# VectorE's share of the attention exponentials, computed on the bit pattern of the bf16 result

## The chip, the cores and the metric

One core of one Trainium2 chip runs the whole program. A time is device microseconds (us) from start to end of one execution. Each execution also lists the mean clock that was granted to TensorE over its span, as a share of full speed; that column matters below. An execution over 1.5% above the fastest of the same kernel counts as slow, and ratios leave it out.

## The reference

```python
x = A_q                                              # 1 x 2048 x 640, bf16
g = sigmoid((x * gate_w).sum(-1, keepdims=True))
a = _A_ref(x, A_k, A_v, ...)    # 4-tap shift of k, times v, long convolution by FFT of length 4096, skip, times q
b = _B_ref(x, wq, wk, wv, wo)   # attention, 32 query heads of 20, one shared key/value head:
#   scores = einsum("bhqd,bkd->bhqk", q, k) * 20 ** -0.5 ;  p = softmax(scores) ;  o = p @ v ;  b = o @ wo
return g * a + (1 - g) * b
```

The attention has 32 x 2048 x 2048 = 134 million scores, each of which needs an exponential. That is what the kernel is built around.

## The kernel before

The kernel is a Python program that lists operations and hands them to a list scheduler of its own. When the kernel is built, this scheduler fixes the order of every engine's instructions, from durations that it models. The stream of score matmuls, exponentials and value matmuls (P times V) has precedence. Everything else is "side work" in its gaps: the convolution (as products with cosine and sine tables), the projections, the output products.

ScalarE takes most exponentials, alternately from three score banks (ETA) and two (ETB):

```python
def EXP(n):
    lo, w = 512 * base[n % 2], 512 * len(units[n])
    op("act", lambda e: e.activation(et(n)[:, 0:w], self.ps[:, lo:lo + w], ACT.Exp, scale=SCALE), ...)
```

VectorE takes 66 pairs of 512-column tiles (a list named DVE_J says which). It evacuates scores as a scaled integer J. The bits of J above the low 16 are the exponent of the result, and the low 16 are the position within the octave, on which a cubic in factored form is computed:

```python
def DEXP(G, j):
    ...
        self.evac(gr, "dve", lambda e, bk, h=h: e.tensor_scalar(        # twice, one per score bank
            J[:, 512 * h:512 * h + 512], self.bank(bk), SCALE * LOG2E * 65536.0, EOFF * 65536.0, ALU.mult,
            ALU.add), (), [kJ], c_ps(512))
    V(lambda e: e.tensor_scalar(E[:, :], J[:, :], 7, 0x7F800000, ALU.logical_shift_left, ALU.bitwise_and), ...)
    V(lambda e: e.scalar_tensor_tensor(Ef, lo, ED, Ef, ALU.add, ALU.mult), ...)
    V(lambda e: e.scalar_tensor_tensor(Jf, lo, EP, lo, ALU.add, ALU.mult), ...)
    V(lambda e: e.scalar_tensor_tensor(T["ETd"][:, :], Jf, EQ, Ef, ALU.add, ALU.mult), ...)
```

One more part matters, and it is in the scheduler. Where nothing is ready for TensorE, it may place a "dummy" matmul. A dummy adds zero weights times anything to the output bank (bank 6), so it changes no result ("fill" and "filler" in the code):

```python
FILL = 0.55
...
if best is None:                                   # no side work is ready for TensorE
    if (self.filler is not None and self.main_started and self.can_fill and m is not None and gap > 0.1
            and self.busy_in(t, 2.4) < FILL):      # modelled activity of the last 2.4 us
        f = Op("pe", self.filler, c_mm(512), "c", "fill", 0.0)
...
if op.name == "pv":
    self.can_fill = not op.last                    # no dummy between the last PV of a group and the next group's first
```

Of the kernel before, what the change touches and what calls it, by code (L numbers as in the profile page):

```python
# [5 lines left out]
dt = mybir.dt  # L6
# [495 lines left out]
CW = 128  # L502
HD = 320

C3 = 0.0780245226404771
ED, EP, EQ = 1.8383391255622578 * 2.0 ** 16, 1.0590468215349557 * 2.0 ** 16, 6.971251820088461 * 2.0 ** 32
EOFF = 127.0 - 48.0 + math.log2(C3)
LOG2E = 1.4426950408889634

UP = 256.0  # L510

# [6 lines left out]
def c_ps(n):  # L518
    return 0.16 + 1.04e-3 * n


def c_fast(n):
    return 0.16 + 0.52e-3 * n
# [10 lines left out]
def c_pool(n):  # L534
    return 0.21 + 1.78e-3 * n
# [6 lines left out]
class Kernel:  # L542
# [59 lines left out]
    def alloc(self):  # L602
# [3 lines left out]
        def sb(name, shape, dtype):  # L606
            T[name] = nc.alloc_sbuf_tensor(name, shape, dtype)
# [29 lines left out]
            sb(f"ETA{i}", [128, 1536], BF16)  # L637
            sb(f"ETB{i}", [128, 1024], BF16)
        sb("ETd", [128, 1024], BF16)
        sb("dJ0", [128, 1024], dt.uint32)  # L640
        sb("dJ1", [128, 1024], dt.uint32)
        sb("dE", [128, 1024], dt.uint32)
        sb("kv", [128, NSC, D], BF16)
        sb("xn", [128, NSC, D], BF16)
        sb("ident", [128, 128], BF16)
# [368 lines left out]
    def attention(self):  # L1014
        T = self.T
        op = self.op
        self.stream()
        units = self.units
        base = (0, 3)
# [39 lines left out]
        def DEXP(G, j):  # L1059

            par = self.ndexp % 2
            self.ndexp += 1
            pr = -600.0 + 0.1 * G + 0.001 * j
            J, E, kJ = T[f"dJ{par}"], T["dE"], ("dJ", par)
            lo = J[:, :].bitcast(dt.uint16).rearrange("p (n t) -> p n t", t=2)[:, :, 0]
            Ef, Jf = E[:, :].bitcast(F32), J[:, :].bitcast(F32)
            k = dict(port=True, name="dexp", prio=pr)
            V = self.dve
            rs = self.on_dve[G, j]
            for h, r in enumerate(rs):  # L1070
                gr = self.group("dqk", pr, banks=(5, 7))
                gr.rides = True

                w = self.g.writer.get(kJ)
                soft = set() if h else set(self.g.readers.get(kJ, ())) | ({w} if w is not None else set())
                self.mm(gr, lambda e, bk, r=r: score(e, bk, G, j, r), [("kT4", j // 4), ("qT", G // 8 % 2, G % 8)],
                        0.04)
                o = gr.mms[0]
                o.row = r
                if self.dqk is not None:  # L1080
                    o.deps.add(self.dqk)
                self.dqk = o
                o.soft = soft - o.deps
                o.deps |= o.soft
                self.evac(gr, "dve", lambda e, bk, h=h: e.tensor_scalar(  # L1085
                    J[:, 512 * h:512 * h + 512], self.bank(bk), SCALE * LOG2E * 65536.0, EOFF * 65536.0, ALU.mult,
                    ALU.add), (), [kJ], c_ps(512))
            V(lambda e: e.tensor_scalar(E[:, :], J[:, :], 7, 0x7F800000, ALU.logical_shift_left, ALU.bitwise_and),  # L1088
              [kJ], ["dE"], c_fast(1024), **k)
            V(lambda e: e.scalar_tensor_tensor(Ef, lo, ED, Ef, ALU.add, ALU.mult), [kJ, "dE"], ["dE"], c_ps(1024),  # L1090
              **k)
            V(lambda e: e.scalar_tensor_tensor(Jf, lo, EP, lo, ALU.add, ALU.mult), [kJ], [kJ], c_ps(1024), **k)  # L1092
            V(lambda e: e.scalar_tensor_tensor(T["ETd"][:, :], Jf, EQ, Ef, ALU.add, ALU.mult), [kJ, "dE"], ["ETd"],  # L1093
              c_ps(1024), **k)

        def PVmm(r, j, src, key, late=False, **k):
            return op("pe", lambda e: e.matmul(  # L1097
                self.bank(6)[32 * r:32 * r + 32, :], T["vaug"][:, j, :], src,
                start=(j == 0), stop=(j == NSC - 1), tile_position=(0, 32 * r)),
                [key, "vaug", ("vaugb", j // 4)], [] if late else [("ps", 6)], name="pv", **k)  # L1100

        def PV(G, j, rs):
            pv0 = None
# [91 lines left out]
    def tail(self):  # L1195

        T = self.T
        acc, g = T["acc"], 7
        v = lambda t: t[:, :].rearrange("p (b r) -> p b r", r=32)
        p = -9000.0  # L1200
        self.dve(lambda e: e.transpose(acc[:, :], self.bank(6)), [("ps", 6)], ["acc"], c_ps(512), prio=p, name="tp")
        self.dve(lambda e: e.reciprocal(T["rcp"][:, :], v(acc)[:, :, 20]), ["acc"], ["rcp"], 0.3, prio=p, name="rcp")
        self.dve(lambda e: e.tensor_tensor(v(T["oTn"]), v(acc), T["rcp"][:, :].unsqueeze(2).to_broadcast([128, 16, 32]),
                                           ALU.mult), ["acc", "rcp"], ["oTn"], c_ps(512), prio=p, port=True,
                 name="onorm")
        self.dve(lambda e: e.transpose(T["oT3"][:, g, :], T["oTn"][:, :]), ["oTn"], [("oT3", g)], c_ps(512), prio=p,
                 name="tp")

        def mm(ci, half, g):
            b, n0 = 2 * ci + half, HD * half  # L1210
            self.op("pe", lambda e: e.matmul(
                self.bank(b, HD), T["oT3"][:, g, 128 * ci:128 * ci + 128], T["wog"][:, g, n0:n0 + HD],
                start=(g == 6), stop=(g == 7)), [("oT3", g), "wog"], [("ps", b)], c_mm(HD), name="op2", main=True,
                banks=(b,))

        def warm():

            self.op("pe", lambda e: e.matmul(self.bank(0, HD), T["zeros"][:, :], T["wog"][:, 6, 0:HD], start=False,
                                             stop=False), ["zeros", "wog"], [("ps", 0)], c_mm(HD), name="warm",
                    main=True, banks=(0,))  # L1220

        for ci in range(4):
            for half in range(2):
                mm(ci, half, 6)
            if ci >= 2:
                for _ in range(6):
                    warm()
        for ci in range(4):
            i = 4 * (NB - 1) + ci
            osb = T[f"outsb{ci}"]  # L1230
            for half in range(2):
                mm(ci, half, 7)
            self.dve(lambda e, ci=ci, i=i, osb=osb: e.scalar_tensor_tensor(
                osb[:, :].rearrange("p (h n) -> p h n", h=2),
                self.ps[:, 1024 * ci:1024 * ci + 1024].rearrange("p (h n) -> p h n", h=2)[:, :, 0:HD],
                T["omgf"][:, i:i + 1], T["part"][:, ci, :].rearrange("p (h n) -> p h n", h=2), ALU.mult, ALU.add),
                ["omgf", ("ps", 2 * ci), ("ps", 2 * ci + 1), ("part", ci)], [("outsb", ci)], c_ps(D), prio=p,
                name="op2_ev")
            self.dma(self.aps["out"][0][128 * i:128 * i + 128, :], osb[:, :], reads=[("outsb", ci)],
                     nbytes=163840, prio=p, name="st_out", eng="act" if ci % 2 else "sp")  # L1240
# [300 lines left out]
```

## Time and profile before

| | before |
|---|---|
| three timed executions | 908.10, 911.01, 912.96 us |
| mean granted clock, profiled execution | 0.998 |
| to the first exponential ("head") | 25.30 us |
| first to last start of an exponential ("stream") | 872.65 us |
| after the last start ("tail") | 9.95 us |
| ACT busy, DVE busy, PE busy | 883.9, 631.9, 853.1 of 907.9 us |
| dummy matmuls in the stream, by their weight loads | 149 |

The prediction shows and reads the lines behind this. In profile lines PE stands for TensorE's matmuls, PEld for its weight loads, DVE for VectorE, ACT for ScalarE, POOL for GpSimd. Three rows add up to the span (head, stream, tail), so any change of time must appear in one of them. The stream is nearly the whole of it. What it takes beyond the undisturbed 854.1 us, which the prediction works out, is called its loss here. A caution: most of these traces lack the matmul records of some dummies (before has 111 for its 149 weight loads), so TensorE's busy time is read a little low where dummies stand.

### The profile page before, as it was taken

Reading aid. Unit: us, or ns where it says so; the run is one execution under the profiler, and the core shown is the slowest. Engines: PE = TensorE matmul, PEld = TensorE weight load, DVE = VectorE, ACT = ScalarE, POOL = GpSimd, SP = SyncE. Lnnn points to the kernel's source line nnn. Section 1 sums busy time; section 2 is a strip of 40 time slices with the busy share of each in tenths; the row PEclk is TensorE's granted clock in tenths of the full one; section 3 lists DMA queues with packets and bytes.
Section 4 is the critical chain, followed back from the end, with each engine's and each line's share of the span. In section 5 each row is a group of like instructions: output and inputs, shape, how many; then the busy total and the mean of one; then the engine's idle time right before and its main releaser. Section 6 shows DMA issues by size and latency. Waiting matters only on the chain.

```text
span 907.9 us, 16333 instructions
## 1 busy us (share of the span) xinstructions
PE 853.1 (94%) x6950; PEld 350.7 (39%) x7013; DVE 631.9 (70%) x878; ACT 883.9 (97%) x791; POOL 380.2 (42%) x330
## 2 busy tenths in 40 slices
PE   6999999999999999999999999999999998998897
PEld 3344344443433344343333333343443332432233
DVE  5446743456766668876887778876678896787964
ACT  5999999999999999999999999999999999999995
POOL 2940056870426396154685213769125495000000
PEclk9999999999999999999999999999999999999999
DMA  7940300010000010000010200000000000301111
GB/s 162 200 134 9 65 19 20 7 37 18 20 19 14 9 41 19 19 19 13 13 37 19 56 20 13 19 8 18 20 19 14 18 4 25 93 13 35 64 35 52
DMA packets 58507, 32.69 MB, mean 36 GB/s; under 512 B 41154, under 2 KB 54466, under 8 KB 58434
## 3 DMA queue, kind: packets, MB, share of 16 engines
q1 hardware_dynamic: 56168, 31.05, 12.7%
q8 instruction: 55, 0.90, 0.4%
q10 hardware_dynamic: 2266, 0.59, 0.3%
q14 instruction: 18, 0.15, 0.1%
HBM read 18.01 MB, written 6.02 MB: 26 GB/s over the span
## 4 chain that ended last, share of the span: by engine, by line
ACT 64%; PE 29%; DMA 3%; SPq 2%; DVE 2%; issue 1%; DVEq 0%
ACT ETA L1055 39%; ACT ETB L1055 25%; PE ps L1023 8%; PE ps L1336 6%; PE ps L1097 6%; PE ps L1400 3%; PE ps L949 2%; PE ps L1270 1%; DMA kTr<-in_A_k_dram 1%; SPq L1253 1%; DMA rbc<-scr_d 1%; DMA xT<-in_A_q_dram 1%; PE ps L1434 1%; PE ps L1187 1%; SPq L722 1%
## 5 line engine op out<-in xcount | busy, mean ns | idle before, releaser
L1055 ACT ACTIVATE ETA<-ps 128x1536 bf16<-128x1536 f32 x384 | 571.3, 1488 | 3.5 <-PE ps L1097 2.2
L1055 ACT ACTIVATE ETB<-ps 128x1024 bf16<-128x1024 f32 x383 | 410.3, 1071 | 0.2 <-PE ps L1023 0.2
L1023 PE MATMUL ps<-qT,kT 21*128 21x512 bf16 x2048 | 302.5, 384 | 34.6 <-ACT ETA L1055 22.7
L1367 POOL TENSOR_TENSOR Pp<-X,K 128x512 f32<-128x512 bf16 x120 | 168.6, 1430 | 358.2 <-DVE K L1355 350.8
L1097 PE MATMUL ps<-ETA,vaug 128*32 128x512 bf16 x1150 | 196.1, 389 | 0.4 <-DVE acc L1151 0.3
L1097 PE MATMUL ps<-ETB,vaug 128*32 128x512 bf16 x766 | 188.1, 389 | 0.0
L1023 PEld LDWEIGHTS ps<-qT,kT 21*128 21x128 bf16 x2048 | 74.7, 91 | 223.2 <-ACT ETA L1055 122.9
L1085 DVE TENSOR_SCALAR dJ<-ps 128x512 uint32<-128x512 f32 x132 | 90.7, 687 | 43.8 <-PE ps L1023 43.4
L1093 DVE SCALAR_TENSOR_TENSOR ETd<-dJ,dE 128x1024 bf16<-128x1024 f32 x66 | 89.4, 1354 | 19.5 <-PE ps L1097 19.4
L1090 DVE SCALAR_TENSOR_TENSOR dE<-dJ,dE 128x1024 f32<-128x1024 uint16 x66 | 89.9, 1362 | 0.5
L1092 DVE SCALAR_TENSOR_TENSOR dJ<-dJ 128x1024 f32<-128x1024 uint16 x66 | 89.3, 1353 | 0.4
L1367 POOL TENSOR_TENSOR AB<-Pp 128x256 bf16<-128x256 f32 x80 | 77.4, 967 | 4.9
L1400 PE MATMUL ps<-AB,Tcos 128*128 128x256 bf16 x320 | 78.2, 275 | 0.8 <-DVE dJ L1085 0.6
L1097 PEld LDWEIGHTS ps<-ETA,vaug 128*32 128x32 bf16 x1150 | 47.7, 93 | 65.6 <-issue 63.0
L1400 PE MATMUL ps<-AB,Tsin 128*128 128x256 bf16 x280 | 69.3, 275 | 0.0
L1097 PEld LDWEIGHTS ps<-ETB,vaug 128*32 128x32 bf16 x766 | 45.3, 92 | 43.5 <-issue 42.9
L1367 POOL TENSOR_TENSOR Pp<-Pp 128x512 f32<-128x512 f32 x40 | 60.9, 1524 | 2.7
L1088 DVE TENSOR_SCALAR dE<-dJ 128x1024 uint32<-128x1024 uint32 x66 | 54.1, 820 | 0.5
L1336 PE MATMUL ps<-ssm_kT,Tsin 128*128 128x256 bf16 x320 | 53.7, 275 | 0.0
L1336 PE MATMUL ps<-kv,Tsin 128*128 128x256 bf16 x320 | 53.7, 275 | 0.0
L1336 PE MATMUL ps<-kv,Tcos 128*128 128x256 bf16 x320 | 52.0, 275 | 1.2 <-DVE kv L1410 0.5
L1336 PE MATMUL ps<-ssm_kT,Tcos 128*128 128x256 bf16 x320 | 51.8, 275 | 0.4 <-DVE dJ L1085 0.3
(135 smaller groups left out, 807.5 us busy)
## 6 DMA issues: line engine op xcount, KB each, us to landing
rbc<-scr_d SPq DMA_DIRECT2D x31, 256.0 KB
scr_o<-oTn SPq DMA_DIRECT2D x24, 128.0 KB, 1.8
xn<-in_A_q_dram SPq DMA_DIRECT2D x4, 640.0 KB
kv<-in_A_v_dram SPq DMA_DIRECT2D x4, 640.0 KB, 5.3
out_dram<-outsb SPq DMA_DIRECT2D x14, 160.0 KB, 1.8
oTp<-scr_o SPq DMA_DIRECT2D x12, 160.0 KB, 5.2
wog<-in_B_wo_dram SPq DMA_DIRECT2D x4, 200.0 KB
wo<-in_B_wo_dram SPq DMA_DIRECT2D x4, 200.0 KB, 3.3
```

The source lines that it names most:

```text
L949: o = self.mm(gr, lambda e, bk, gi=gi, dc=dc: e.matmul(self.bank(bk), T["wq_pad"][:, dc, 128 * gi:128 * gi + 128], T["xT"][:, dc, 512 * I: ...
L1023: return e.matmul(self.bank(bk), T["kT4"][32 * r:32 * r + 21, 128 * j:128 * j + 128], T[f"qT{G // 8 % 2}"][32 * r:32 * r + 21, G % 8, :], ...
L1055: op("act", lambda e: e.activation(et(n)[:, 0:w], self.ps[:, lo:lo + w], ACT.Exp, scale=SCALE), [("ps", base[n % 2] + k) for k in range(le ...
L1085: self.evac(gr, "dve", lambda e, bk, h=h: e.tensor_scalar(J[:, 512 * h:512 * h + 512], self.bank(bk), SCALE * LOG2E * 65536.0, EOFF * 6553 ...
L1088: V(lambda e: e.tensor_scalar(E[:, :], J[:, :], 7, 0x7F800000, ALU.logical_shift_left, ALU.bitwise_and), [kJ], ["dE"], c_fast(1024), **k)
L1090: V(lambda e: e.scalar_tensor_tensor(Ef, lo, ED, Ef, ALU.add, ALU.mult), [kJ, "dE"], ["dE"], c_ps(1024), **k)
L1092: V(lambda e: e.scalar_tensor_tensor(Jf, lo, EP, lo, ALU.add, ALU.mult), [kJ], [kJ], c_ps(1024), **k)
L1093: V(lambda e: e.scalar_tensor_tensor(T["ETd"][:, :], Jf, EQ, Ef, ALU.add, ALU.mult), [kJ, "dE"], ["ETd"], c_ps(1024), **k)
L1097: return op("pe", lambda e: e.matmul(self.bank(6)[32 * r:32 * r + 32, :], T["vaug"][:, j, :], src, start=(j == 0), stop=(j == NSC - 1), ti ...
L1336: o = self.mm(gr, lambda e, bk, lhs=lhs, rhs=rhs, comp=comp, n=n: e.matmul(self.bank(bk, 256, 256 * comp), lhs, rhs, start=(n == 0), stop= ...
L1367: f = lambda e: e.tensor_tensor(out, a, b, alu)
L1400: self.mm(gr, lambda e, bk, lhs=lhs, fc=fc, comp=comp, h=h: e.matmul(self.bank(bk, 256, 256 * h), lhs, AB[:, fc, :, comp, :], start=(fc == ...
```

## The change

The intent is to shorten VectorE's chain from four links after the evacuations to three. The evacuation writes a negative f32, W = 128 x (score in octaves + 44) - 32768. Rounded to int16, W is already a bf16 bit pattern with the sign bit set: an exponential whose fraction is interpolated linearly, negative and too small by 2^83. What is missing is a cubic correction in the position within the octave, and that position can be read off the low 16 bits of W as a float. So shift-and-mask goes. The sign and the 2^83 are made good by a second value tile, vneg, which the products with VectorE's results load in place of vaug.

```diff
+DA = -10.141843429407468 / 2.0 ** 48
+DP = -5.834910002780118 * 2.0 ** 16
+DQ = 4.8360429603910475 * 2.0 ** 32
+KDN = 83
...
+        self.pool(lambda e: e.tensor_scalar(T["vneg"][:, :, :], T["vaug"][:, :, :], -(2.0 ** KDN), 1.0, ALU.mult,
+                                            ALU.mult), ...)
...
-                    J[:, 512 * h:512 * h + 512], self.bank(bk), SCALE * LOG2E * 65536.0, EOFF * 65536.0, ALU.mult,
-                    ALU.add), (), [kJ], c_ps(512))
-            V(lambda e: e.tensor_scalar(E[:, :], J[:, :], 7, 0x7F800000, ALU.logical_shift_left, ALU.bitwise_and),
-            V(lambda e: e.scalar_tensor_tensor(Ef, lo, ED, Ef, ALU.add, ALU.mult), [kJ, "dE"], ["dE"], c_ps(1024),
-            V(lambda e: e.scalar_tensor_tensor(Jf, lo, EP, lo, ALU.add, ALU.mult), [kJ], [kJ], c_ps(1024), **k)
-            V(lambda e: e.scalar_tensor_tensor(T["ETd"][:, :], Jf, EQ, Ef, ALU.add, ALU.mult), [kJ, "dE"], ["ETd"],
+                    W[:, 512 * h:512 * h + 512], self.bank(bk), SCALE * LOG2E * 128.0,
+                    128.0 * (127 - KDN) - 32768.0, ALU.mult, ALU.add), (), [kW], c_ps(512))
+            V(lambda e: e.scalar_tensor_tensor(X[:, :], w, DP, w, ALU.add, ALU.mult), [kW], ["dX"], c_ps(1024), **k)
+            V(lambda e: e.scalar_tensor_tensor(X[:, :], X[:, :], DQ, w, ALU.add, ALU.mult), [kW], ["dX"], c_ps(1024),
+            V(lambda e: e.scalar_tensor_tensor(T["ETd"][:, :].bitcast(dt.int16), X[:, :], DA, W[:, :], ALU.mult,
+                                               ALU.add), [kW, "dX"], ["ETd"], c_ps(1024), **k)
...
+            va = "vneg" if late else "vaug"
-                self.bank(6)[32 * r:32 * r + 32, :], T["vaug"][:, j, :], src,
+                self.bank(6)[32 * r:32 * r + 32, :], T[va][:, j, :], src,
...
+            if g == 6 and ci == 0 and half == 0:         # first output matmul of the tail
+                o.deps.update(x for gr in self.g.groups for x in gr.evacs)
```

The scheduler works from durations, so removing one instruction also moves nearly every side matmul a little, and the dummies with them.

More of the change, by code (lines that the diff above doesn't have):

```diff
@@ L503 @@
 HD = 320
-C3 = 0.0780245226404771
-ED, EP, EQ = 1.8383391255622578 * 2.0 ** 16, 1.0590468215349557 * 2.0 ** 16, 6.971251820088461 * 2.0 ** 32
-EOFF = 127.0 - 48.0 + math.log2(C3)
 LOG2E = 1.4426950408889634
+DA = -10.141843429407468 / 2.0 ** 48
+DP = -5.834910002780118 * 2.0 ** 16
+DQ = 4.8360429603910475 * 2.0 ** 32
+KDN = 83
 UP = 256.0
@@ L639, in alloc @@
         sb("ETd", [128, 1024], BF16)
-        sb("dJ0", [128, 1024], dt.uint32)
-        sb("dJ1", [128, 1024], dt.uint32)
-        sb("dE", [128, 1024], dt.uint32)
+        sb("dW0", [128, 1024], F32)
+        sb("dW1", [128, 1024], F32)
+        sb("dX", [128, 1024], F32)
+        sb("vneg", [128, NSC, 32], BF16)
         sb("kv", [128, NSC, D], BF16)
@@ L1016, in attention @@
         op = self.op
+        self.pool(lambda e: e.tensor_scalar(T["vneg"][:, :, :], T["vaug"][:, :, :], -(2.0 ** KDN), 1.0, ALU.mult,
+                                            ALU.mult), ["vaug"] + [("vaugb", b) for b in range(NB)], ["vneg"],
+                  c_pool(512), prio=14.0, name="vneg", after=self.crow0)
         self.stream()
@@ L1063, in DEXP @@
             pr = -600.0 + 0.1 * G + 0.001 * j
-            J, E, kJ = T[f"dJ{par}"], T["dE"], ("dJ", par)
-            lo = J[:, :].bitcast(dt.uint16).rearrange("p (n t) -> p n t", t=2)[:, :, 0]
-            Ef, Jf = E[:, :].bitcast(F32), J[:, :].bitcast(F32)
+            W, X, kW = T[f"dW{par}"], T["dX"], ("dW", par)
+            w = W[:, :].bitcast(dt.uint16).rearrange("p (n t) -> p n t", t=2)[:, :, 0]
             k = dict(port=True, name="dexp", prio=pr)
@@ L1072, in DEXP @@
                 gr.rides = True
-                w = self.g.writer.get(kJ)
-                soft = set() if h else set(self.g.readers.get(kJ, ())) | ({w} if w is not None else set())
+                wr = self.g.writer.get(kW)
+                soft = set() if h else set(self.g.readers.get(kW, ())) | ({wr} if wr is not None else set())
                 self.mm(gr, lambda e, bk, r=r: score(e, bk, G, j, r), [("kT4", j // 4), ("qT", G // 8 % 2, G % 8)],
@@ L1085, in DEXP @@
                 self.evac(gr, "dve", lambda e, bk, h=h: e.tensor_scalar(
-                    J[:, 512 * h:512 * h + 512], self.bank(bk), SCALE * LOG2E * 65536.0, EOFF * 65536.0, ALU.mult,
-                    ALU.add), (), [kJ], c_ps(512))
-            V(lambda e: e.tensor_scalar(E[:, :], J[:, :], 7, 0x7F800000, ALU.logical_shift_left, ALU.bitwise_and),
-              [kJ], ["dE"], c_fast(1024), **k)
-            V(lambda e: e.scalar_tensor_tensor(Ef, lo, ED, Ef, ALU.add, ALU.mult), [kJ, "dE"], ["dE"], c_ps(1024),
-              **k)
-            V(lambda e: e.scalar_tensor_tensor(Jf, lo, EP, lo, ALU.add, ALU.mult), [kJ], [kJ], c_ps(1024), **k)
-            V(lambda e: e.scalar_tensor_tensor(T["ETd"][:, :], Jf, EQ, Ef, ALU.add, ALU.mult), [kJ, "dE"], ["ETd"],
-              c_ps(1024), **k)
+                    W[:, 512 * h:512 * h + 512], self.bank(bk), SCALE * LOG2E * 128.0,
+                    128.0 * (127 - KDN) - 32768.0, ALU.mult, ALU.add), (), [kW], c_ps(512))
+            V(lambda e: e.scalar_tensor_tensor(X[:, :], w, DP, w, ALU.add, ALU.mult), [kW], ["dX"], c_ps(1024), **k)
+            V(lambda e: e.scalar_tensor_tensor(X[:, :], X[:, :], DQ, w, ALU.add, ALU.mult), [kW], ["dX"], c_ps(1024),
+              **k)
+            V(lambda e: e.scalar_tensor_tensor(T["ETd"][:, :].bitcast(dt.int16), X[:, :], DA, W[:, :], ALU.mult,
+                                               ALU.add), [kW, "dX"], ["ETd"], c_ps(1024), **k)
         def PVmm(r, j, src, key, late=False, **k):
+            va = "vneg" if late else "vaug"
             return op("pe", lambda e: e.matmul(
-                self.bank(6)[32 * r:32 * r + 32, :], T["vaug"][:, j, :], src,
+                self.bank(6)[32 * r:32 * r + 32, :], T[va][:, j, :], src,
                 start=(j == 0), stop=(j == NSC - 1), tile_position=(0, 32 * r)),
-                [key, "vaug", ("vaugb", j // 4)], [] if late else [("ps", 6)], name="pv", **k)
+                [key, va, ("vaugb", j // 4)], [] if late else [("ps", 6)], name="pv", **k)
         def PV(G, j, rs):
@@ L1210, in mm @@
             b, n0 = 2 * ci + half, HD * half
-            self.op("pe", lambda e: e.matmul(
+            o = self.op("pe", lambda e: e.matmul(
                 self.bank(b, HD), T["oT3"][:, g, 128 * ci:128 * ci + 128], T["wog"][:, g, n0:n0 + HD],
```

## The prediction

> **What bounds the kernel now.** The kernel computes attention exponentials on two engines. ScalarE takes most of them, alternately three score banks at once (tile ETA, 1536 columns) and two (ETB, 1024); VectorE takes 66 pairs of score tiles (two of 512 columns each) by integer arithmetic. A long convolution, the projections and the output products are fitted around that as side work. So the first question is which engine sets the pace. I read the busy shares and the slices first.
>
> ```profile
> PE 853.1 (94%) x6950; PEld 350.7 (39%) x7013; DVE 631.9 (70%) x878; ACT 883.9 (97%) x791; POOL 380.2 (42%) x330
> ...
> DVE  5446743456766668876887778876678896787964
> ACT  5999999999999999999999999999999999999995
> ```
>
> ACT is at 90% or more in every slice except the first and last. DVE is at 90% in one slice only (the 33rd, 726 to 749 us). Next the chain that ended last, and the costliest groups:
>
> ```profile
> ACT 64%; PE 29%; DMA 3%; SPq 2%; DVE 2%; issue 1%; DVEq 0%
> ...
> L1055 ACT ACTIVATE ETA<-ps 128x1536 bf16<-128x1536 f32 x384 | 571.3, 1488 | 3.5 <-PE ps L1097 2.2
> L1055 ACT ACTIVATE ETB<-ps 128x1024 bf16<-128x1024 f32 x383 | 410.3, 1071 | 0.2 <-PE ps L1023 0.2
> ...
> L1085 DVE TENSOR_SCALAR dJ<-ps 128x512 uint32<-128x512 f32 x132 | 90.7, 687 | 43.8 <-PE ps L1023 43.4
> L1093 DVE SCALAR_TENSOR_TENSOR ETd<-dJ,dE 128x1024 bf16<-128x1024 f32 x66 | 89.4, 1354 | 19.5 <-PE ps L1097 19.4
> L1090 DVE SCALAR_TENSOR_TENSOR dE<-dJ,dE 128x1024 f32<-128x1024 uint16 x66 | 89.9, 1362 | 0.5
> L1092 DVE SCALAR_TENSOR_TENSOR dJ<-dJ 128x1024 f32<-128x1024 uint16 x66 | 89.3, 1353 | 0.4
> ...
> L1088 DVE TENSOR_SCALAR dE<-dJ 128x1024 uint32<-128x1024 uint32 x66 | 54.1, 820 | 0.5
> ```
>
> The chain runs over ACT and the TensorE steps that feed it; VectorE has 2% of it. The 767 exponentials of line 1055 wait visibly for only 3.7 us. VectorE, in contrast, waits for TensorE before many of its own steps (43.4 us before the evacuations of line 1085 alone): it has room.
>
> The waits hide one thing: these records overlap (571.3 + 410.3 = 981.6 us is more than the span), so a late start may show as lost overlap instead of idle time. I therefore took the start times of all 767 from the timeline. The first is at 25.30 us and the last at 897.95, so the stream takes 872.65 us. The commonest step from an ETA to the next ETB is 1.33 us, and from an ETB to the next ETA 0.90. With 383 of each and no disturbance, it would take 383 x 2.23 = 854.1 us. So 18.6 us are lost inside the stream, nearly all ahead of an ETA (the ETB-to-ETA steps sum to 360.85 us, against 383 x 0.90 = 344.7). That is all that anything outside ScalarE can give back there.
>
> How much of it is VectorE's fault? I looked at the whole-run waits and at the worst step of the stream, in the timeline around 790 us:
>
> ```profile
> PE ps L1400 <- DVE dJ L1085: 0.6, 1, 0.6
> PE ps L1336 <- DVE dJ L1085: 0.6, 2, 0.3
> ...
> 787.81 1.22 DVE L1092 SCALAR_TENSOR_TENSOR dJ<-dJ 128x1024 f32<-128x1024 uint16 x1
> 788.95 0.68 DVE L1085 TENSOR_SCALAR dJ<-ps 128x512 uint32<-128x512 f32 x1
> ...
> 789.69 0.28 PE L1400 MATMUL ps<-AB,Tcos 128*128 128x256 bf16 x1 [0.64 <-DVE dJ L1085]
> ...
> 791.21 1.45 ACT L1055 ACTIVATE ETA<-ps 128x1536 bf16<-128x1536 f32 x1 [0.74 <-PE ps L1097]
> ```
>
> Here VectorE is behind: it finishes a polynomial step, then evacuates a bank; TensorE waits 0.64 us for that bank, the attention matmuls queued behind it come late, and ScalarE stands for 0.74 us. So the mechanism by which VectorE can slow the end exists. But it is rare: all matmul waits for VectorE between 25 and 900 us (those two rows and seven smaller ones, of 0.2 to 0.5) sum to 3.6 us.
>
> **What the Trainium skill says.** *ScalarE: Activation LUTs*, section "What ACT_TABLE_LOAD costs", gives 0.833 ns per element for any function. The trace agrees: (1.33 - 0.90) us over 512 columns is 0.84 ns. The change doesn't touch this floor. *VectorE: DVE Perf Modes*, section "The perf-mode tier table", gives tensor_scalar on fp32 in SBUF the double rate and tensor_tensor on fp32 the single one; it has no row for scalar_tensor_tensor. The 820 ns of line 1088 against about 1355 ns of the three others, all over 1024 four-byte results, fit that scalar_tensor_tensor runs at the single rate. So the instruction removed is the cheapest of the chain. *GPSIMD Engine Reference*, section "8. Key points", says GpSimd shares its SBUF interfaces with VectorE and contends with VectorE's two-port modes and two-SBUF-input instructions. The trace fits: line 1093 ranges from 1.16 to 2.22 us, median 1.22, and one GpSimd table step of 128x511 took 3.52 us beside a VectorE product of 2.81 us, against 0.71 alone. So the means hold contention, and the three remaining polynomial steps keep theirs.
>
> **The change part by part.**
> 1. Two evacuations per pair stay (132 in all, 512 columns). They write f32 instead of uint32, the same four bytes, from the same source. Lines 1151 (f32 copy, 690 ns) and 598 (bf16, 687) show that the output type doesn't move the 687 ns. Cost 0.
> 2. Shift-and-mask (line 1088) goes: 66 x 0.820 = 54.1 us less.
> 3. Three scalar_tensor_tensor stay three. Types change (uint16 with two-element stride as first and second input; f32 with uint16; f32 with f32 into int16), but the old rows with uint16 inputs (1362, 1353) and with f32 inputs and a two-byte result (1354) cost the same. Cost 0.
> 4. The chain keeps its serial shape, four links after the evacuations becoming three: one pair is ready 0.8 us sooner.
> 5. The negative factor moves into a second value tile, vneg, one GpSimd tensor_scalar over 512 bf16: about 0.71 us, by the 128x511 rows of line 809. In the built order it stands before three weight copies needed for the projection of later query groups; one query group lasts 16 x 4 / 5 x 2.24 = 29 us on ScalarE and the first two are ready, so those copies, done by 33.5 us in the trace, have tens of microseconds. Cost 0 on the path.
> 6. The matmuls on VectorE's results load vneg instead of vaug, the same size. Cost 0. Dummy matmuls fall from 149 to 144; all other counts are equal on every engine.
> 7. In the tail the first output matmul now waits for the last VectorE evacuation. Before, this matmul started at 899.02 and that evacuation ended at 898.80 + 0.55 = 899.35. The 20 matmuls from there to the one that needs VectorE's transposed result (ready at 901.73) took to about 901.7, so a start 0.35 us later makes TensorE last by about 0.3: +0.3 us.
>
> VectorE's sum is 631.9 - 54.1 = 577.8 us, about 64%. Beside ScalarE that is hidden. On the path, VectorE's lag can return at most 3.6 us, and not all: TensorE often waits for VectorE because matmuls come close together, not because of line 1088. I take half, 1.8. With the tail: -1.8 + 0.3 = -1.5, so 911.0 - 1.5 = 909.5 us.
>
> **The rivals.**
> - *VectorE's time counts*: all 54.1 us or a good part come off, 857 to 890 us. For it speaks only the 70% and the busy 33rd slice. Against it: ScalarE's own floor. 25.30 us before the stream, 854.1 without any loss, 9.95 after it make 889.4, and the timed runs are 3.1 us longer than this profile: 892.5 us even if every loss in the stream vanished, barely 2% under 911.0.
> - *The new order hurts TensorE*: a scheduler fixes the order in advance, with modelled durations, and nearly every side matmul moves a little. TensorE is 94% busy; attention matmuls that just miss their slot cost ScalarE about 0.15 us each, and that is most of the 18.6 us. Another arrangement may lose 14 or 24 us: 906 to 916. Both directions are open, and it is larger than my 1.8; it sets my range.
> - *Type conversion slows VectorE* (int16 output, or a strided uint16 as both inputs): 0.5 us on each of 66 x 3 steps would add 99 us, to about 677 us of 908, 75%. Nothing in the rows hints at it, and still ScalarE would bound; a few microseconds at most, 912 to 918.
> - *Clock*: granted 0.998, nothing to gain.
>
> **Range and chances.** The three timed runs spread from 908.1 to 913.0, and the rearrangement is worth up to 5 either way, so 904.5 to 914.5. Faster by over 2% needs under 892.8, practically the loss-free stream: 0.01. Slower by over 2% needs 18 us of new loss in an order of the same work: 0.015. Within 2%: 0.975.
>
> **What would show it.** Line 1088's group gone, the evacuations still near 687 ns, the three polynomial steps near 1355, DVE near 578 us. ScalarE still near 884 us with its stream about 872 us long. VectorE's idle time up by about what its busy time falls: waits for TensorE before the evacuations and before the result buffer grow. It would be wrong if the commonest steps (1.33 and 0.90) changed, if ScalarE's stream lost under 10 or over 28 us, or if matmuls began to wait for VectorE's result tile.

## The result, and the profile after

A ratio here is the mean time of one kernel's fast runs over that of the other's fast runs of the same rounds, so it is not quite the ratio of the medians.

| | before | after |
|---|---|---|
| median (range), us | 910.38 (908.1 to 912.96) | 920.62 (920.35 to 922.19) |
| ratio, 95% interval | | 1.0121 (1.0098 to 1.0143): within 2%, yet clearly slower |
| profiled span | 907.9 | 918.7 |
| head, stream, tail | 25.30, 872.65, 9.95 | 23.41, 885.06, 10.23 |
| mean granted clock, all four runs | 0.998 (profiled) | 0.983, 0.984, 0.984, 0.983 |

The predicted range ended at 914.5, so the prediction missed. The increase of 10.8 us between the profiled runs is +12.41 in the stream, +0.28 in the tail and -1.89 in the head. (Heads of 23.4 to 26.8 us occur across all the kernels here.)

First the busy shares, two rows of the slices and the chain's engines, after:

```profile
PE 863.1 (94%) x6947; PEld 353.9 (39%) x7008; DVE 579.9 (63%) x812; ACT 885.6 (96%) x791; POOL 366.8 (40%) x331
...
ACT  5999999999999999999999999999999999999785
PEclk9999999999999999999999999999999999999589
...
ACT 62%; PE 32%; SPq 2%; DMA 2%; DVE 1%; issue 0%; DVEq 0%
```

The row of the granted clock before, which the prediction did not show:

```profile
PEclk9999999999999999999999999999999999999999
```

VectorE has lost its 52 us, as intended. The news is in the 38th slice and its neighbour: the clock falls to half there, and ScalarE, at 90% or more in all slices but the outermost before, has a 7 and an 8.

The groups after (busy us, mean ns of one | idle before, and the wait that ended most of it):

```profile
L1062 ACT ACTIVATE ETA<-ps 128x1536 bf16<-128x1536 f32 x384 | 569.3, 1483 | 13.7 <-PE ps L1030 7.5
L1062 ACT ACTIVATE ETB<-ps 128x1024 bf16<-128x1024 f32 x383 | 407.6, 1064 | 0.6 <-PE ps L1030 0.5
...
L1091 DVE TENSOR_SCALAR dW<-ps 128x512 f32<-128x512 f32 x132 | 90.7, 687 | 43.2 <-PE ps L1030 42.4
L1097 DVE SCALAR_TENSOR_TENSOR ETd<-dX,dW 128x1024 int16<-128x1024 f32 x66 | 90.2, 1366 | 26.2 <-PE ps L1102 26.0
L1094 DVE SCALAR_TENSOR_TENSOR dX<-dW 128x1024 f32<-128x1024 uint16 x66 | 88.4, 1339 | 0.4
L1095 DVE SCALAR_TENSOR_TENSOR dX<-dX,dW 128x1024 f32<-128x1024 f32 x66 | 86.0, 1303 | 0.3
```

No instruction of the new arithmetic costs more than its predecessor by over 12 ns (1366 against 1354). ScalarE's exponentials last no longer either, but they wait 13.7 us instead of 3.5 before an ETA.

Where does it wait? From the starts of all exponentials, the loss of the stream over its 854.1 us can be split. Before, it is 0.43 us between 848 and 880 us and 18.13 elsewhere. After, it is **11.94 us in the same stretch** and 19.03 elsewhere. One stretch of 32 us holds nearly the whole difference. The stretch by windows, after (window, us, busy time of PE, PEld, DVE, ACT and POOL with their instructions, granted clock, DMA share, GB/s):

```profile
840.00:844.00 4.00, 3.20 (x24) 1.09 (x23) 3.97 (x5) 4.00 (x5) 0.00 (x0) 1.00 0.25 82
844.00:848.00 4.00, 2.75 (x23) 0.77 (x24) 2.39 (x5) 4.00 (x5) 0.00 (x0) 0.95 0.27 84
848.00:852.00 4.00, 3.77 (x19) 0.94 (x19) 3.44 (x5) 2.64 (x3) 0.00 (x0) 0.50 0.15 47
...
872.00:876.00 4.00, 4.00 (x19) 1.31 (x17) 1.10 (x2) 2.47 (x3) 0.00 (x0) 0.50 0.01 4
...
880.00:884.00 4.00, 4.00 (x32) 1.53 (x30) 1.95 (x4) 4.00 (x5) 0.00 (x0) 1.00 0.00 0
```

The same place before:

```profile
844.00:848.00 4.00, 3.39 (x31) 1.05 (x29) 3.97 (x6) 4.00 (x5) 0.00 (x0) 1.00 0.15 45
```

After, TensorE is busy only 2.75 of the 4 us from 844 (3.39 before). At 847.6 us its clock falls to half and returns at 878.3. From 848 to 880 TensorE is busy 31.2 of the 32 us and is the bound, while ScalarE works only 21.9 of them. After 880 all is normal again.

What makes the thin stretch is seen in the timeline of TensorE. After:

```profile
844.10 0.39 PE L1030 MATMUL ps<-qT,kT 21*128 21x512 bf16 x3 [0.32 <-ACT ETA L1062]
...
845.02 0.39 PE L1030 MATMUL ps<-qT,kT 21*128 21x512 bf16 x3 [0.20 <-ACT ETB L1062]
846.36 0.39 PE L1030 MATMUL ps<-qT,kT 21*128 21x512 bf16 x3 [0.95 <-ACT ETA L1062]
```

Before:

```profile
843.34 0.38 PE L1482 MATMUL ps<-Tcos,zeros 128*128 128x512 bf16 x1 [0.16 <-issue]
...
844.36 0.39 PE L1482 MATMUL ps<-Tcos,zeros 128*128 128x512 bf16 x1
844.58 0.43 PE L1434 MATMUL ps<-wo,oTp 128*128 128x320 bf16 x2
```

Before, dummies (the rows with zeros) and two output products stand between the score matmuls. After, there is nothing for 0.95 us. By their weight loads, the 4 us from 844 hold one dummy and five output products before; after, they hold no dummy, and three output products that come only from 847.2 on. In the new order the hand-over of the output bank from one query group to the next falls here, and dummies are forbidden there because they would write to that bank. The bank of the output products is no help, as VectorE evacuates it only at 846.15. The page's count "149 before, 144 after" shows nothing of this.

### The profile page after: what moved, and what is told of

The parts are those of the page before. It is cut to its first block, busy times and chain, and to the rows that moved or that the text cites. A ratio compares the mean times of both kernels' runs of the same rounds, so it can differ in the third digit from the quotient of the medians.

```text
span 918.7 us, 16261 instructions
## 1 busy us (share of the span) xinstructions
PE 863.1 (94%) x6947; PEld 353.9 (39%) x7008; DVE 579.9 (63%) x812; ACT 885.6 (96%) x791; POOL 366.8 (40%) x331
## 4 chain that ended last, share of the span: by engine, by line
ACT 62%; PE 32%; SPq 2%; DMA 2%; DVE 1%; issue 0%; DVEq 0%
ACT ETA L1062 38%; ACT ETB L1062 24%; PE ps L1030 9%; PE ps L1343 8%; PE ps L1102 7%; PE ps L1407 3%; PE ps L953 2%; SPq L1260 1%; PE ps L1441 1%; DMA kTr<-in_A_k_dram 1%; PE ps L969 1%; DMA xT<-in_A_q_dram 1%; PE ps L1192 1%; PE ps L1489 1%; SPq L726 1%; DVE ETd L1097 0%
## 5 line engine op out<-in xcount | busy, mean ns | idle before, releaser
L1062 ACT ACTIVATE ETA<-ps 128x1536 bf16<-128x1536 f32 x384 | 569.3, 1483 | 13.7 <-PE ps L1030 7.5
L1030 PE MATMUL ps<-qT,kT 21*128 21x512 bf16 x2048 | 306.1, 389 | 36.0 <-ACT ETA L1062 23.1
L1374 POOL TENSOR_TENSOR Pp<-X,K 128x512 f32<-128x512 bf16 x120 | 156.2, 1327 | 365.6 <-DVE K L1362 361.1
L1102 PE MATMUL ps<-ETB,vaug 128*32 128x512 bf16 x766 | 190.3, 394 | 0.0
L1091 DVE TENSOR_SCALAR dW<-ps 128x512 f32<-128x512 f32 x132 | 90.7, 687 | 43.2 <-PE ps L1030 42.4
L1097 DVE SCALAR_TENSOR_TENSOR ETd<-dX,dW 128x1024 int16<-128x1024 f32 x66 | 90.2, 1366 | 26.2 <-PE ps L1102 26.0
L1094 DVE SCALAR_TENSOR_TENSOR dX<-dW 128x1024 f32<-128x1024 uint16 x66 | 88.4, 1339 | 0.4
L1095 DVE SCALAR_TENSOR_TENSOR dX<-dX,dW 128x1024 f32<-128x1024 f32 x66 | 86.0, 1303 | 0.3
L1156 DVE COPY acc<-ps 128x512 f32<-128x512 f32 x31 | 21.4, 690 | 54.8 <-PE ps L1102 54.8
L1343 PE MATMUL ps<-ssm_kT,Tsin 128*128 128x256 bf16 x320 | 51.5, 275 | 0.0
```

The lines of the kernel that those rows point to most:

```text
L1030: return e.matmul(self.bank(bk), T["kT4"][32 * r:32 * r + 21, 128 * j:128 * j + 128], T[f"qT{G // 8 % 2}"][32 * r:32 * r + 21, G % 8, :], ...
L1091: self.evac(gr, "dve", lambda e, bk, h=h: e.tensor_scalar(W[:, 512 * h:512 * h + 512], self.bank(bk), SCALE * LOG2E * 128.0, 128.0 * (127 ...
L1094: V(lambda e: e.scalar_tensor_tensor(X[:, :], w, DP, w, ALU.add, ALU.mult), [kW], ["dX"], c_ps(1024), **k)
L1095: V(lambda e: e.scalar_tensor_tensor(X[:, :], X[:, :], DQ, w, ALU.add, ALU.mult), [kW], ["dX"], c_ps(1024), **k)
L1097: V(lambda e: e.scalar_tensor_tensor(T["ETd"][:, :].bitcast(dt.int16), X[:, :], DA, W[:, :], ALU.mult, ALU.add), [kW, "dX"], ["ETd"], c_ps ...
L1102: return op("pe", lambda e: e.matmul(self.bank(6)[32 * r:32 * r + 32, :], T[va][:, j, :], src, start=(j == 0), stop=(j == NSC - 1), tile_p ...
```

## The experiments

The theory after reading the traces (theory C in the expectations): *the arithmetic is innocent; the new order leaves a thin stretch for TensorE, there the clock falls to half, and that is the loss.* The rivals: the new instructions (int16 result, vneg) disturb something (theory A); or the new order as such costs about 10 us at full clock (theory O). Some edits below set the dummy threshold for a stretch of the scheduler's modelled time, which is some microseconds off the chip's. The mean clock is known for every run, but the place of a fall only for the one profiled run of each kernel. "Correct" below says that the kernel's output agreed with the reference, not that an expectation came true. Runs of the old arithmetic, run 3 excepted, carry the change's added dependency of the first tail matmul too. A new threshold changes the scheduler's order after the first place where it acts, and not only the dummies.

**1. Eight more dummies ahead of the fall, all else as after.**

```diff
-                    and self.busy_in(t, 2.4) < FILL):
+                    and self.busy_in(t, 2.4) < (0.7 if 830 < t < 838 else FILL)):
```

> The changed kernel with 8 more dummy matmuls, placed only in the stretch ahead of the clock drop (the scheduler's threshold for dummies is raised there alone; the order up to there is unchanged). Theory C (the thin stretch of TensorE work at 844 to 847 us lets the granted clock fall to 0.5 for some 30 us, and that costs the 10 us): no drop, clock 0.998, about 909 us. Theory O (the new order loses slots, whatever the clock): still about 920.

Correct. Median 916.86 us, ratio 1.0077 (1.0021 to 1.0134). Two runs stayed at clock 0.996 to 0.998 and took 911.57 and 912.89; two were at 0.984 and took 920.84 and 921.18. The profiled run is one of the latter:

```profile
666.00:670.00 4.00, 2.94 (x29) 0.89 (x27) 4.00 (x6) 4.00 (x5) 0.00 (x0) 1.00 0.04 8
670.00:674.00 4.00, 3.75 (x19) 1.26 (x18) 3.68 (x6) 3.69 (x4) 0.00 (x0) 0.60 0.15 60
...
844.00:848.00 4.00, 3.21 (x27) 0.94 (x24) 4.00 (x6) 4.00 (x5) 0.00 (x0) 1.00 0.00 0
```

With the dummies TensorE is busy 3.21 us from 844, and the clock holds there. But it fell elsewhere, at 670.8 us, after another thin window (2.94 of 4). So this is half a miss: the place was mended, the cause is not a single place. The runs at full clock speak for the theory: the new arithmetic in nearly its own order then costs 911.6 to 912.9, not 920.6.

**2. Before without shift-and-mask, rescheduled.** It gives a wrong result on purpose: old evacuation, old types, no vneg.

```diff
-            V(lambda e: e.tensor_scalar(E[:, :], J[:, :], 7, 0x7F800000, ALU.logical_shift_left, ALU.bitwise_and), ...
-            V(lambda e: e.scalar_tensor_tensor(Ef, lo, ED, Ef, ALU.add, ALU.mult), ...
+            V(lambda e: e.scalar_tensor_tensor(Ef, lo, ED, lo, ALU.add, ALU.mult), ...
(and the added dependency of the first tail matmul, as in the change)
```

> The kernel before with the shift-and-mask step alone left out (the result is wrong on purpose; no vneg, no int16 output; bits as integers). The scheduler then thins out TensorE at the same place as in the changed kernel. Theory C: a clock drop near the same place, about 918 to 921 us. Theory A (the new arithmetic, types or vneg cost the time): about 910, as before.

Median 918.13 us, ratio 1.0096 (1.0045 to 1.0148), clocks 0.979 to 0.994; in the profiled run TensorE is busy 2.53 of the 4 us from 844, the clock falls at 848.0 and is back at 871.9. The loss and its place appear with none of the new instructions, so they are not needed for it. What this kernel shares with the changed one is left: VectorE's shorter chain, and the order that the scheduler makes of it. Run 3 separates the two.

**3. Before in its exact order, shift-and-mask on two columns only.** Wrong on purpose again. The scheduler is still told the old duration, so nothing moves, but VectorE is relieved.

```diff
-            V(lambda e: e.tensor_scalar(E[:, :], J[:, :], 7, 0x7F800000, ALU.logical_shift_left, ALU.bitwise_and),
+            V(lambda e: e.tensor_scalar(E[:, 0:2], J[:, 0:2], 7, 0x7F800000, ALU.logical_shift_left, ALU.bitwise_and),
...
-            V(lambda e: e.scalar_tensor_tensor(Ef, lo, ED, Ef, ALU.add, ALU.mult), ...
+            V(lambda e: e.scalar_tensor_tensor(Ef, lo, ED, lo, ALU.add, ALU.mult), ...
```

> The kernel before in exactly its own order on every engine, but the shift-and-mask works on 2 columns instead of 1024 (wrong result on purpose): VectorE is relieved of some 50 us and nothing moves. This is the step of the prediction that took 1.8 us for VectorE's relief, by itself. By that step: 908.5, 0 to 3.6 us less than before. If relief is worth nothing: 910.4, ratio 1.000. The clock should not drop, 0.998.

Ratio 1.0010 (0.9974 to 1.0046). The three runs at clock 0.998 or more took 907.59, 908.9 and 909.61 us (mean 908.7), beside a mean of 908.5 for the five runs of before at such a clock; a fourth fast run, at 0.992, took 913.07. Relief alone is worth nothing that can be measured, though the interval is 2.4 us less to 4.2 us more and so doesn't exclude the predicted 1.8. One further run took 931.77 at clock 0.961; it is a slow run and enters no comparison, but its profile shows that the old order too, with VectorE sped up, is not safe from a fall (68 us at half clock, from 822.5).

**4. Before with three dummies fewer near 826 us.** This is the converse of run 1: old arithmetic, 146 dummies instead of 149.

```diff
-                    and self.busy_in(t, 2.4) < FILL):
+                    and self.busy_in(t, 2.4) < (0.0 if 826 < t < 834 else FILL)):
```

> The kernel before with 3 dummy matmuls fewer in one short stretch near 826 us (a right result); arithmetic and VectorE's steps as before. Theory C: the stretch is then as thin as the one in the changed kernel, the clock drops there, and the time goes to about 918 to 922. Theory O: within 1 us of before.

Correct. Median 923.2 us, ratio 1.0104 (1.0028 to 1.0180). One run held its clock (0.997) and took 910.79; the others had 0.966 to 0.975 and 922.83 to 929.2. The profiled run:

```profile
830.00:834.00 4.00, 2.85 (x27) 0.93 (x27) 3.13 (x5) 4.00 (x4) 0.00 (x0) 1.00 0.11 41
834.00:838.00 4.00, 3.87 (x23) 1.03 (x20) 3.05 (x5) 3.28 (x4) 0.00 (x0) 0.52 0.00 0
```

TensorE is busy 2.85 of 4 us where the three dummies were (3.95 before), and the clock falls right behind. Taking three idle-looking matmuls out of the kernel before makes it some 14 us slower in most runs; one of these, 929.2, counts as slow and is left out of the ratio.

**5. After with dummies kept dense everywhere.** The threshold is raised to 0.75, and dummies may also go into a free side bank while the output bank changes hands; 306 dummies.

```diff
-FILL = 0.55
+FILL = 0.75
...
+            if (self.filler7 is not None and self.main_started and not self.can_fill and m is not None and gap > 0.1
+                    and self.busy_in(t, 2.4) < FILL):
+                for b in (7, 5):
+                    if not self.bank_claimed[b] and not self.bank_busy[b] and self.bank_ready[b] <= t:
+                        f = Op("pe", lambda e, b=b: self.filler7(e, b), c_mm(512), "c", "fill", 0.0)
...
```

> The changed kernel with dummy matmuls allowed until TensorE is three quarters busy (306 of them instead of 144), also into a free side bank when the output bank is being handed over, so that no stretch is thin. Theory C: the clock stays at 0.996 or above in every run, 909 to 912 us. Theory O (the order itself, or the dummies, cost the time): 915 or more at full clock.

Correct. Median 911.84 us (911.17 to 912.99), ratio 1.0027 (1.0003 to 1.0051), all four clocks 0.998 to 1.000.

```profile
844.00:848.00 4.00, 4.00 (x31) 1.41 (x31) 3.42 (x6) 4.00 (x4) 0.00 (x0) 1.00 0.12 41
```

TensorE is never thin, the clock does not fall, and about 9 of the 10 us are back with the arithmetic unchanged. The stream takes 874.95 us, 2.3 more than before: no more than that is lost in this order once the clock holds.

**6. After once more.**

> The changed kernel once more, on this chip and in these rounds. If its thin stretch is thin enough to let the clock fall whenever it is run: clock 0.983 and 920 us in all runs. If the fall is a matter of chance: some runs at 0.997 and 909 to 912.

Four runs: 912.99 us at clock 0.996, 921.34 at 0.983, and two slow ones, 931.74 at 0.971 and 934.62 at 0.964. The ratio over the two fast runs is 1.0084 (1.0020 to 1.0148). The same program, in the same order, can keep its clock or lose it once or more, and its time goes with that. The profiled run, 934.62, fell twice: at 671.6 us, where run 1 fell too, and at 859.4, behind the thin stretch of the hand-over, which came some 12 us later after the first fall. The thin place makes the fall likely, not certain; the section on the prediction says what else decides.

**7. After with the threshold at 0.60.** It has 189 dummies (45 more, and 3 more ahead of the stream), but the thin stretch near 844 us stays as thin as it was: over 3.4 us, TensorE's busy share there is 0.57, in both kernels their lowest.

```diff
-FILL = 0.55
+FILL = 0.60
```

> The changed kernel with the threshold for dummies raised from 0.55 to 0.60: 48 more dummy matmuls over the whole run, but none in the thin stretch ahead of the drop, which stays as thin. Theory C in its narrow form (the thinnest stretch decides): the clock still falls near 845 to 850 us, about 920. If the mean activity decides: no fall, about 910.

Correct. Median 912.66 us, ratio 1.0041 (1.0012 to 1.0070), clocks 0.993 to 1.000, no fall in the profiled run. This is a miss for the narrow form of the theory, "the thinnest 3.4 us alone decides". For the profiled run the traces give a reason, a grid of time on which the stretch lay otherwise; it is shown in the section on the prediction. Whether the added dummies also helped the three other runs, for which only a mean clock is known, stays open.

**8 and 9. The room put to use.** VectorE has 52 us free that nobody uses. So more pairs were given to it, with dense dummies: 70 pairs (threshold 0.78), then 75 pairs at places found by trying many in the scheduler (threshold 0.70, 241 dummies).

```diff
-DVE_J = [(), (), (), (), (), (6,), (2, 9), (2, 9), (2, 9), ...     # 66 pairs
+DVE_J = [(), (), (), (5,), (), (5, 11), (2, 6), (1, 5, 9), ...     # 75 pairs (run 9)
```

> The changed kernel with dense dummies (threshold 0.78) and 70 pairs on VectorE instead of 66: four pairs of 1024 columns taken off ScalarE at 0.84 ns each, 3.4 us. Theory C: clock at 0.996 or above, 3 to 4 us less than e5_dense, 905 to 908 us, a little faster than before. If TensorE has no room for the extra dummies and pairs: as e5_dense or slower.

> The changed arithmetic with dense dummies (threshold 0.70) and 75 pairs, redistributed over the groups by a search over the scheduler's orders: nine pairs of 1024 columns off ScalarE at 0.84 ns each, 7.7 us against e5_dense (911.8). If freed VectorE time pays only as moved pairs: 902 to 905 us, clock 0.996 or above, faster than before by 0.5 to 1%. If TensorE or VectorE becomes the bound: 908 or more.

Both correct. 70 pairs: 905.47 us, ratio 0.9959 (0.9934 to 0.9984). 75 pairs: **902.09 us** (901.63 to 902.51), ratio 0.9917 (0.9903 to 0.9932), clock 0.999 to 1.000. The latter beats both kernels. Its page:

```profile
PE 871.0 (97%) x7044; PEld 359.0 (40%) x7114; DVE 626.0 (70%) x857; ACT 875.7 (97%) x783; POOL 381.9 (42%) x331
```

VectorE is at 70% again, as before the change, and ScalarE has 875.7 us of work instead of 885.6. Nine pairs are 18 tiles of 512 columns; at 0.84 ns a column (from the steps 1.33 and 0.90) that is 7.7 us of it; the eight instructions fewer (783 against 791) are probably the rest.

**10. The same 75 places with the old arithmetic.**

```diff
(run 9 with the changed arithmetic undone, everything else kept)
```

> The same 75 pairs in the same places, dense dummies, but with the old arithmetic (shift-and-mask kept): VectorE has 75 x 0.82 = 61 us more to do. If the freed time is what lets the pairs move: clearly slower than e9_75pairs, 920 to 940 us, with side work left over after the last exponential. If not: within 2 us of it.

Correct. 935.72 us at clock 0.999 to 1.000, ratio 1.0289 (1.0272 to 1.0306). The last exponential starts at 900.54 us and 33.3 us follow, against a tail of 9.95 before: side work was left over. So at those places VectorE's four-link chain is too long, and there the removed instruction counts: 33.6 us of time (935.72 - 902.09) for about 61 us of VectorE's work.

**11. The old arithmetic, 66 pairs, with run 5's dense dummies** (threshold 0.75, 294 dummies).

> The old arithmetic, 66 pairs, with the dense dummies of e5_dense. Theory C with relief worth nothing: the same as e5_dense, 910 to 913 us, at clock 0.996 or above. If the 2.5 us that e5_dense lies above before come from the new arithmetic: 908 to 910.

Correct. 916.24 us, ratio 1.0077 (1.0053 to 1.0101), where 910 to 913 was expected: a miss. The one run at clock 1.000 took 911.33, those at 0.994 to 0.996 took 915 to 917, those at 0.987 to 0.988 took 920.0 to 921.72. The profiled run fell twice, at 690.1 to 700.4 and 720.9 to 734.5 us. TensorE was busy 2.82 of the last 3.4 us before the first fall, 2.32 of 3.4 before the second. Dense dummies do not exclude falls. The time again follows the clock.

**12. Before with the threshold at 0.35:** 35 dummies in the stream instead of 149.

```diff
-FILL = 0.55
+FILL = 0.35
```

> The kernel before, old arithmetic, threshold for dummies 0.35 instead of 0.55: about 120 dummies fewer, many stretches as thin as the changed kernel's. Theory C: the clock falls several times per run, mean clock under 0.97, 930 us or more. If dummies don't matter: 908 to 910.

Correct. 996.77 us (976.94 to 1009.4), clock 0.854 to 0.894. Beside the fastest, the three others count as slow, so there is no ratio of fast runs, and only the order of size is taken from it: the dummies, which compute nothing, hold up tens of microseconds. Its row of the clock:

```profile
PEclk8799999779999889999788997779996895955589
```

Falls are now everywhere, and a row like this is what to look for.

Two more runs were made for what was still open: whether the place of the fall can be chosen, and what the arithmetic is worth when both sides are tuned.

**13. Run 5 with a hole** in the dummies between 500 and 560 us of modelled time (277 left).

```diff
-                    and self.busy_in(t, 2.4) < FILL):
+                    and self.busy_in(t, 2.4) < (0.3 if 500 < t < 560 else FILL)):
```

> e5_dense, whose clock never fell, with the dummies held back (threshold 0.30) for 60 us only, about 505 to 570 us of the execution; 29 dummies fewer, the rest of the rules unchanged. Theory C: the clock falls there or within 5 us after, and nowhere else in the stream; clock below 0.99 in most runs, 918 us or more. If the fall is tied to the place near 847 us or to the last conv and output steps: no fall, 912.

Correct. 922.91 us, ratio 1.0143 (1.0094 to 1.0191), all four clocks 0.973 to 0.989. The profiled run:

```profile
510.00:515.00 5.00, 3.34 (x30) 1.09 (x27) 4.46 (x7) 5.00 (x5) 0.00 (x0) 1.00 0.04 14
515.00:520.00 5.00, 4.73 (x27) 1.35 (x25) 0.81 (x3) 3.69 (x4) 0.00 (x0) 0.51 0.09 30
...
540.00:545.00 5.00, 3.73 (x34) 1.30 (x32) 4.44 (x6) 5.00 (x6) 0.00 (x0) 1.00 0.13 52
545.00:550.00 5.00, 4.71 (x28) 1.47 (x28) 4.34 (x7) 4.39 (x4) 0.10 (x1) 0.58 0.08 26
```

A place where no other profile of this arithmetic shows a fall now has two, each right behind a thin window. The hole was chosen; the falls followed. A third one, at 859.9 us, was not expected; it lies behind a thin window too (2.89 of the 4 us from 856, against 3.95 in run 5), as the hole also moved what came after it.

**14. The old arithmetic with its own searched places:** 70 pairs, threshold 0.75, 277 dummies.

> The old arithmetic with its own best found order: dense dummies and 70 pairs, redistributed by the same search that gave e9_75pairs for the new arithmetic (the search found no order with more than 71 that ends as early). If what the new arithmetic buys is room for five more pairs: 905 to 908 us at full clock, some 4 us above e9_75pairs (902.1). If it buys nothing: 902.

Correct. 907.04 us, ratio 0.9968 (0.9954 to 0.9982). So with both sides tuned, the new arithmetic is at 902.1 and the old at 907.0, in terms of before 0.9917 and 0.9968: about half a per cent. The search was short on both sides, and the pair of numbers holds only for these two kernels.

## Why the prediction was wrong

The prediction's steps, against what was measured:

- *ScalarE bounds; VectorE's saved time is hidden.* Right. DVE measured 579.9 us (577.8 predicted), ACT 885.6 (about 884), and VectorE's waits grew: before the copies of the output bank (line 1151, now 1156) from 39.4 to 54.8 us, before the result buffer from 19.4 to 26.0.
- *Steps 1 to 5: evacuations, types, vneg.* Right. 687 ns, polynomial steps 1339, 1303 and 1366 ns, vneg 0.617 us at 24.5 us, off the path. Run 2 shows the loss without any of them. (One reading was wrong, without consequence: of the three polynomial steps at about 1355 ns, that of line 1093 writes bf16 results, not four-byte ones.)
- *Step 7, the tail.* Right: +0.28 us against +0.3.
- *Relief, -1.8 us.* Not shown either way: run 3 measured none, but only within about 3 us (0.36% of 909). It is small beside what was missed.
- *Step 6, "Cost 0. Dummy matmuls fall from 149 to 144".* **This is the step that failed.** It counted the dummies and the other matmuls ("all other counts are equal") instead of asking where they lie. In the new order TensorE has neither a dummy nor side work for 0.95 us before 846.36, its busy time from 844 falls from 3.39 to 2.75 of 4 us, and a cost of 0 became a half clock of 30.7 us.
- *The rival "Clock: granted 0.998, nothing to gain".* This is the same error seen from the other side. It asked only whether the clock could rise. Losing it cost 11.94 - 0.43 = 11.5 us of stream.
- *The rival "the new order hurts TensorE", 906 to 916.* It was the right family with the wrong mechanism. At full clock, the order costs 0.9 us outside the stretch (19.03 against 18.13) and at most 2.3 in run 5. The prediction's range allowed only for matmuls that miss their slots, so it ended at 914.5. Its last clause did name the sign, a stream that loses over 28 us: it lost 31.0. (Another of its signs came in part: TensorE's waits for VectorE's result tile grew from 0.8 to 4.1 us over the whole run.)

So the sum that the prediction should have had is about +0.9 for the order elsewhere, +0.3 for the tail, 0 for relief, and +11.5 for one fall of the clock, where it had 0. With the head's -1.9, which varies between executions, that makes the 10.8 us between the two profiles.

What is shown: the loss sits in the stretch of half clock (the two traces); it comes with the order, without the new instructions (run 2), and not with relief alone (run 3's fast runs); one and the same program is slow or fast as its clock falls or holds (run 6); taking dummies out makes falls at the place chosen (runs 4 and 13), putting them in removes the one at 848 (the profiles of runs 1 and 5). *TensorE: Matmul & The Clock Gate* in the Trainium skill, section "Part 1: The HAM clock gate (the "warmup" mystery)", describes such a gate: two states, one at half rate, chosen by how busy the array has been in a free-running window of about 3.4 us. The traces agree on the half rate (0.50 in the windows of the fall), and on the window. In each of the 16 profiles, all changes of the clock lie a whole number of times 3.41 us apart (78 changes, none off by more than 0.002 us), and the place of this grid differs from execution to execution.

So TensorE's busy share has to be taken in the windows of each execution's own grid. For the thin stretches above:

| profile | window on its grid, us | TensorE busy of 3.40 us | then |
|---|---|---|---|
| after | 844.20 to 847.60 | 2.25 | fall |
| run 2 | 844.60 to 848.00 | 2.25 | fall |
| run 4 | 830.80 to 834.20 | 2.25 | fall |
| run 6, same program as after | 855.90 to 859.30 | 1.93 | fall |
| run 7, the same thin stretch | 842.90 to 846.30, 846.30 to 849.70 | 2.87, 2.47 | none |

In run 7 the thin stretch, 0.57 busy in itself, lay across two windows, and neither was so thin. All 16 profiles together, in the stream and at full clock, with a missing dummy's record put back as 0.38 us at its weight load: all 11 windows under a share of 0.69 were followed by a fall, 16 of 143 between 0.69 and 0.85, and none of some 3800 above. That one program falls in three runs and not in a fourth (run 6) fits a grid that runs free of it.

What stays open is what decides between 0.69 and 0.85, and how long a fall lasts: 24 to 48 us after and in runs 1, 2, 4 and 6, 68 in run 3's slow run, at most 14 in the dense orders of runs 11, 13 and 14, but anything from 3.4 to 51 in run 12, which has the fewest dummies.

## What to carry to other kernels

When a schedule is changed, read the granted clock and TensorE's busy time window by window (3.4 us long here, and anywhere on the time axis, since the grid moves), in the thinnest places above all; a count of instructions, or a mean clock of 0.998 before, says nothing of how near to a fall the kernel is. Work that looks idle, as these dummies do, may hold up 10 us and more, so check what each of them is next to before you call their number unimportant. And an engine that is relieved beside the bound gives nothing until it is given work of the bound: the saved 52 us were worth nothing at 66 pairs, and with the clock secured they paid for nine more pairs and 902.1 us. Of that, about half a per cent is the new arithmetic's own (run 14); the rest, dense dummies and searched places, the old arithmetic can have too.

## What the Trainium skill lacked or had wrong

- *TensorE: Matmul & The Clock Gate*, section "Why this matters for your kernels", advises "No PE-idle gaps >~3µs between matmul bursts". That was too weak here. The longest gap in the stretch ahead of the fall was 0.95 us; a window with TensorE busy 2.53 to 2.94 of 4 us was enough, though not in every run. The busy share of a window on the 3.41 us grid, not the longest gap, was the better warning. (The page also tells of a kernel in which frequent short idle times made the clock swing, but gives no share.)
- The same page, "Part 1", has the clock return after at least one busy window of about 3.4 us. Here one was seldom enough. In the fall after the change TensorE showed no idle time from 868 to 876 us and was still at 0.50. The falls lasted 30.7 us after the change, 27.3 in run 1, 23.9 in run 2, 47.8 in run 4; only one of three in run 13 and one of fourteen in run 12 lasted a single window. What a window needs for the return, the page doesn't say.
- *VectorE: DVE Perf Modes*, section "The perf-mode tier table", has no row for scalar_tensor_tensor, and no page gives a time for it. Over 1024 elements of 128 partitions it took 1.22 us undisturbed (the medians are 1217 to 1224 ns), the same for f32, for uint16 with a stride of two as input and for an int16 or bf16 result; the means of 1303 to 1366 ns hold contention.
